# Attention stage of a two-layer mixture kernel: order of the operand splits, spread of the score matmuls, number format of the second mix, engine of the remainders

## The chip, the cores and the metric

One core of a Trainium2 chip runs the whole program. The metric is device time in microseconds (us): the median of several executions. The profile is of one more execution, read by the hardware profiler. Engines: TensorE (PE, its weight loads PEld), VectorE (DVE), ScalarE (ACT), GpSimd (POOL), and SyncE (SP), which here only issues transfers (DMAs).

## What is computed

Attention with mixing over heads, then two feed-forward layers. Batch 4, 12 heads, 448 positions, head size 64. Cut to what matters here:

```python
scores = scale * np.matmul(q, k.transpose(0, 1, 3, 2))
scores = np.einsum('bhij,hg->bgij', scores, w_pre)      # first mix, over heads
attn = np.exp(scores - np.max(scores, axis=-1, keepdims=True))
attn = attn / (np.sum(attn, axis=-1, keepdims=True) + 1e-09)
attn = np.einsum('bgij,gk->bkij', attn, w_post)         # second mix
return np.matmul(attn, v)                               # then x @ w_in, tanh, @ w_out, experts
```

Inputs are float32. The kernel keeps float32 accuracy by writing an operand as a 16-bit high part and a 16-bit remainder and adding up products of the parts.

## The kernel before

The change lies in `attention` alone. What it does is cut into 180 **steps**, 45 for each of the four batches b. A step takes ten query positions with all twelve heads, 120 rows. A batch has four tiles of queries (`TILES`, t = 0 to 3) of 12, 12, 12 and 9 steps; a step is (b, t, c), and its number is 45 b + 12 t + c.

For step s the program writes, in this order:

- `shuffle` (L220): a transfer `G<-S` that gathers the 120 rows of the step out of the score tile S. SP runs its list in order, and four G buffers rotate (`GB`), so the transfer for step s + 4 can start when the first mix of step s has read its G.
- `premix` (L236): the first mix on TensorE (L240, float32, two passes, 120x448), the row minimum on VectorE (L244), for a halved step a bias add (L248), the exponential on ScalarE with its row sum (L250). A **halved** step (`halved`, L90) scales its exponentials, and GpSimd makes the 16-bit remainder of them (L255).
- whatever `at(s, ...)` put down for step s (the table `todo`): `scores`, and the loading and splitting of operands.
- `after` (L391): every second step `normalise` (L258: add an epsilon L265, reciprocal L266, then the second mix's weights `wr`, one instruction L272 for a float32 step, two, L276 and L277, for a halved one), then `postmix` (L281) of step s - 4 (`LAG`): the second mix on TensorE (L290: 8 matmuls in float32 or 12 in 16 bits), the copy out of PSUM on ScalarE (L294), the remainder on GpSimd (L295).

`scores(b, t, p)` (L195) makes the scores of two heads for a whole tile, six matmuls (L203), and copies them to S: one copy in three on VectorE (L207), the others on ScalarE (L209). Six such calls make a tile, p = 0 to 5; they run while the tile before is being mixed (L388).

Operands are loaded into one pool of three buffers, `raw` (`p3`):

- v of a batch, four parts: `fetch_v` (L183), then `split_v` (L186): the high part on ScalarE (L192), the remainder on GpSimd (L193), 128x768.
- q and k of the next batch, three double pairs of heads: `fetch_pairs` (L168) and `split_pairs` (L179): per load a high part on ScalarE (L175, 128x896) and two remainders (L177, 128x448), one on VectorE and one on GpSimd.
- the first feed-forward weights, `fetch_w` and `convert_w` (three conversions and a remainder on VectorE, L77 to L81 and L327).

When a batch's last step is mixed, `window` (L355) runs `values` (L298): 24 matmuls for each two heads, about 14 us of TensorE, with conversions of weights between. The window of batch b stands behind step 45 (b + 1) + 3.

PSUM banks: scores 0 and 1, first mix 2, 3 and 6 in turn, second mix and values 4 and 5. The five exponential tiles A rotate too (`LAG + 1`).

The order on each engine is not that of the text: a scheduler orders the instructions at compile time by its own estimates and the dependencies, and each engine then runs its list strictly in order. Code behind the attention stage is the same in both kernels, and so is its order from the last steps of batch 3 on.

## Time and profile before

| | us |
|---|---|
| median of 3 runs | 1286.94 (1285.57 to 1294.75) |
| the profiled execution | 1288.26 |
| its span, first to last instruction | 1286.0 |
| TensorE busy | 1193.8 (93%) |
| VectorE busy | 855.1 (66%) |
| ScalarE busy | 729.0 (57%) |
| GpSimd busy | 707.3 (55%) |

The attention stage takes the first 470 us. How to read the rows below: a stretch A:B is in us from the first instruction; `(x310)` counts instructions; PEclk is the granted TensorE clock as a share of full speed; in a timeline, the bracket at the end of a row is the engine's idle time just before it and what ended it. A busy TensorE is modelled and holds its pipelining; start to start is its pace.

### The profile page before, as it was taken

The page shows a single profiled execution, that of the slowest core. Times are in us where ns is not written, and L with a number is a line of the kernel's source. Part 1 is how long each engine was busy: PE and PEld are TensorE (multiplying, and loading weights), DVE is VectorE, ACT ScalarE, POOL GpSimd, SP SyncE. Part 2 cuts the span into 40 slices and gives each one's busy share as a digit, 9 for nine tenths or more (in the row PEclk, how much of TensorE's full clock was granted, in tenths as well). Part 3 has the DMA queues.
Part 4 walks back from the last instruction along what each step waited for, and adds up shares of the span by engine and source line. Part 5 has one row for each costly group of instructions (what it writes and reads, how often), then busy time and mean ns, then how long its engine had stood idle before and what let it go on. Part 6 is the DMA issues. An engine that isn't in the chain of part 4 may idle for free.

```text
span 1286.0 us, 23742 instructions
## 1 busy us (share of the span) xinstructions
PE 1193.8 (93%) x8624; PEld 837.4 (65%) x8648; DVE 855.1 (66%) x1895; ACT 729.0 (57%) x1499; POOL 707.3 (55%) x594
## 2 busy tenths in 40 slices
PE   8999899989999988999899999999978899999995
PEld 3655565555555664566566666667876678989883
DVE  5877687768767829977766456745878345566662
ACT  6777687667767744444455444545556334555551
POOL 5887678577767753433443335334566355566550
PEclk8999999999999999999999999999998999999998
DMA  6555746555574476223001000100043656678640
GB/s 212 174 182 146 221 162 190 175 182 184 148 208 162 116 236 219 93 97 131 25 1 50 1 25 1 50 1 1 2 140 133 212 194 205 213 242 263 229 159 22
DMA packets 82854, 173.90 MB, mean 135 GB/s; under 512 B 12155, under 2 KB 60155, under 8 KB 82728
## 3 DMA queue, kind: packets, MB, share of 16 engines
q1 hardware_dynamic: 76986, 160.75, 38.7%
q0 software_dynamic: 5472, 11.43, 3.0%
q8 instruction: 70, 1.15, 0.4%
q14 instruction: 56, 0.46, 0.1%
q10 hardware_dynamic: 270, 0.12, 0.0%
HBM read 110.79 MB, written 23.30 MB: 104 GB/s over the span
## 4 chain that ended last, share of the span: by engine, by line
PE 59%; DVE 16%; DMA 12%; ACT 6%; issue 3%; POOL 2%; SPq 0%; POOLq 0%; ACTq 0%; DVEq 0%
PE bank L561 11%; PE bank L533 10%; PE bank L913 7%; PE bank L240 7%; PE bank L937 7%; PE bank L290 7%; DMA G<-S 3%; PE bank L203 3%; DMA raw_v<-in_v_dram 3%; PE bank L305 2%; DVE g L547 2%; DMA wor<-in_w_out_dram 2%; DVE g L548 2%; DVE wl_a L903 2%; ACT A L250 1%
## 5 line engine op out<-in xcount | busy, mean ns | idle before, releaser
L561 PE MATMUL bank<-ghl,whl 128*128 128x512 f32 (+1 forms) x1152 | 258.1, 376 | 9.3 <-POOL ghl L551 4.9
L561 PEld LDWEIGHTS bank<-ghl,whl 128*128 128x128 f32 x1152 | 199.6, 192 | 50.8 <-POOL ghl L551 6.3
L483 POOL TENSOR_TENSOR whl<-wo,whl 128x768 fp32r<-128x768 f32 x64 | 118.8, 1857 | 177.2 <-ACT whl L482 177.1
L295 POOL TENSOR_TENSOR at<-at 128x480 f16<-128x480 f32 x180 | 177.0, 996 | 51.9 <-ACT at L294 50.2
L240 PE MATMUL bank<-G,wmix 120*120 120x448 f32 x360 | 176.7, 575 | 11.3 <-DMA G<-S 11.3
L290 PE MATMUL bank<-wr,A 120*128 120x120 f32 (+4 forms) x1800 | 175.3, 246 | 5.2 <-ACT x L312 3.0
L250 ACT ACTIVATE A<-bank,st 120x448 f32<-120x448 f32 x180 | 114.3, 636 | 53.5 <-DVE st L244 22.2
L244 DVE TENSOR_REDUCE st<-bank 120x1 f32<-120x448 f32 x180 | 111.2, 618 | 46.3 <-PE bank L240 45.1
L903 POOL TENSOR_TENSOR wl_a<-wr_a,wh_a 128x768 bf16<-128x768 f32 x56 | 93.1, 1670 | 70.4 <-ACT wh_a L902 70.0
L551 POOL TENSOR_TENSOR ghl<-g,ghl 128x512 fp32r<-128x512 f32 (+1 forms) x64 | 76.6, 1197 | 99.7 <-ACT ghl L550 99.7
L903 DVE TENSOR_TENSOR wl_a<-wr_a,wh_a 128x768 bf16<-128x768 f32 x56 | 83.1, 1484 | 61.9 <-ACT wh_a L902 61.9
L533 PEld LDWEIGHTS <-wih 128*128 128x128 f16 x768 | 72.4, 99 | 76.3 <-issue 15.9
L290 PEld LDWEIGHTS bank<-wr,A 120*128 120x128 f32 (+1 forms) x720 | 94.5, 198 | 34.5 <-issue 17.8
L294 ACT COPY at<-bank 128x480 f32<-128x480 f32 x180 | 101.3, 567 | 25.0 <-PE bank L290 24.7
L902 ACT CAST wh_a<-wr_a 128x768 f16<-128x768 f32 x112 | 92.6, 829 | 39.2 <-PE bank L937 35.2
L543 DVE SCALAR_TENSOR_TENSOR g<-bank,u 128x512 f32<-128x512 f32 (+1 forms) x64 | 39.9, 623 | 108.6 <-ACT d L540 105.2
L255 POOL TENSOR_TENSOR A<-A 120x448 f16<-120x448 f32 (+1 forms) x90 | 84.4, 938 | 32.0 <-ACT A L250 13.4
L482 ACT CAST whl<-wo 128x768 fp32r<-128x768 f32 x64 | 53.1, 831 | 71.1 <-PE bank L561 53.0
L533 PE MATMUL bank<-mxh,wih 128*128 128x512 f16 (+1 forms) x384 | 85.1, 358 | 5.4 <-DVE d L544 4.2
L290 PEld LDWEIGHTS <-A 120*128 120x128 bf16 (+2 forms) x1080 | 63.1, 100 | 40.9 <-issue 33.9
L550 ACT CAST ghl<-g 128x512 fp32r<-128x512 f32 (+1 forms) x64 | 36.2, 566 | 91.6 <-DVE g L548 81.0
L913 PE MATMUL bank<-xph_a,wh_a 128*128 128x208 f16 (+5 forms) x336 | 87.2, 262 | 0.0
(214 smaller groups left out, 2701.3 us busy)
## 6 DMA issues: line engine op xcount, KB each, us to landing
wr_a<-in_w_dram SPq DMA_DIRECT2D x64, 768.0 KB
G<-S SPq DMA_DIRECT2D x176, 210.0 KB
raw_w<-in_w_in_dram SPq DMA_DIRECT2D x32, 384.0 KB
wor<-in_w_out_dram SPq DMA_DIRECT2D x16, 768.0 KB
raw_v<-in_v_dram SPq DMA_DIRECT2D x16, 384.0 KB
yg<-row SPq DMA_DIRECT2D x3, 1540.0 KB
raw_q<-in_q_dram SPq DMA_DIRECT2D x9, 448.0 KB
raw_k<-in_k_dram SPq DMA_DIRECT2D x9, 448.0 KB
```

Of the source, the lines that this page charges most:

```text
L240: nc.tensor.matmul(ps[:r, :S], wmix[:r, :r], g[:r], start=True, stop=True)
L244: nc.vector.tensor_reduce(out=st[:r, k:k + 1], in_=ps[:r, :S], axis=AX.X, op=ALU.min)
L250: nc.scalar.activation(out=a[:r, :S], in_=ps[:r, :S], func=AF.Exp, bias=bias, scale=-1.0, accum_out=st[:r, 4 + k:5 + k])
L290: nc.tensor.matmul(ps[:, jc * r:jc * r + r], x[:r, js], w[:r].rearrange("p (a b) -> p a b", b=10)[:, :, :n], start=(i == 0), stop=(i == le ...
L294: nc.scalar.copy(at32[:, :, t0:t0 + n], v)
L295: nc.gpsimd.tensor_tensor(out=atl[:, :, t0:t0 + n], in0=at32[:, :, t0:t0 + n], in1=ath[:, :, t0:t0 + n], op=ALU.subtract)
L483: nc.gpsimd.tensor_tensor(out=w[:, 1], in0=wo[f], in1=w[:, 0].bitcast(F32), op=ALU.subtract)
L533: nc.tensor.matmul(h, u[f][:, c], X[b][v][:, c, :N], start=(i == 0), stop=(i == len(seq) - 1))
L561: nc.tensor.matmul(Y[b][c][:, :N], w[:, u, 128 * c:128 * c + 128], hl[:, v, :N], start=(f == 0 and i == 0), stop=(f == FC - 1 and i == 2))
L902: nc.scalar.copy(wh, raw)
L903: (nc.vector if j else nc.gpsimd).tensor_tensor(out=wl, in0=raw, in1=wh, op=ALU.subtract)
L913: nc.tensor.matmul(h, w[u][:, 128 * c:128 * c + 128], XP[e][v][:, c, :N], start=(i == 0), stop=(i == len(seq) - 1))
```

## The change

1. `halved`: two steps in three (all but every third) instead of every second are mixed a second time in 16 bits; the table of epsilons has six columns instead of two.
2. `split` and `split_v`: all remainders of loaded q, k and v go to VectorE; before, GpSimd made half of those of q and k, and all of v.
3. `behind`: the splits of v, q, k and the conversions of weights are tied behind the row minimum and the exponential of the step in whose slot they stand (`latest`), and they come first in the slot. Two loads (`fetch_v`, `fetch_pairs`) come four steps ahead of their split; before, that was four for v and two for q and k. Splits of v move from steps 5, 9, 13, 17 of a batch to 9, 13, 17, 21; those of q and k from 25, 29, 33 to 27, 31, 35.
4. `scores` of the next tile lie within eight steps of a tile of twelve (two steps ahead of the tile to six behind its start) instead of twelve; the gathering transfers may start three steps ahead of a tile instead of two.

```diff
 def halved(u):
-    return u % 2 == 1
+    return u % 3 != 0
@@ split
-            for p, eng in enumerate((nc.vector, nc.gpsimd)):
-                eng.tensor_tensor(out=lo[:, 2 * u + p, s0:], in0=raw[:, p], in1=hi[:, 2 * u + p, s0:], op=ALU.subtract)
+            for p in range(2):
+                nc.vector.tensor_tensor(out=lo[:, 2 * u + p, s0:], in0=raw[:, p], in1=hi[:, 2 * u + p, s0:],
+                                        op=ALU.subtract)
@@ split_v
-            nc.gpsimd.tensor_tensor(out=vl[:, jc], in0=raw, in1=vh[:, jc], op=ALU.subtract)
+            nc.vector.tensor_tensor(out=vl[:, jc], in0=raw, in1=vh[:, jc], op=ALU.subtract)
@@ premix
-            nc.vector.tensor_reduce(out=st[:r, k:k + 1], in_=ps[:r, :S], axis=AX.X, op=ALU.min)
+            latest["dve"] = nc.vector.tensor_reduce(out=st[:r, k:k + 1], in_=ps[:r, :S], axis=AX.X, op=ALU.min)
-            nc.scalar.activation(out=a[:r, :S], in_=ps[:r, :S], func=AF.Exp, bias=bias, scale=-1.0,
-                                 accum_out=st[:r, 4 + k:5 + k])
+            latest["act"] = nc.scalar.activation(out=a[:r, :S], in_=ps[:r, :S], func=AF.Exp, bias=bias, scale=-1.0,
+                                                 accum_out=st[:r, 4 + k:5 + k])
@@ the table of steps
+        def behind(f, *a):
+            with ExitStack() as order:
+                for x in latest.values():
+                    order.enter_context(tc.issue_after(x.ins))
+                f(*a)
-                at(s0 + 1 + 4 * jc, fetch_v, b, jc)
-                at(s0 + 5 + 4 * jc, split_v, b, jc)
+                at(s0 + 9 + 4 * jc, behind, split_v, b, jc)
+                at(s0 + 5 + 4 * jc, fetch_v, b, jc)
+                    at(s0 + 27 + 4 * u, behind, split_pairs, b + 1, u)
                     at(s0 + 23 + 4 * u, fetch_pairs, b + 1, u)
-                    at(s0 + 25 + 4 * u, split_pairs, b + 1, u)
-                at(45 * b + 10 + 7 * k, fetch_w, u)
-                at(45 * b + 13 + 7 * k, convert_w, u)
+                at(45 * b + 7 + 7 * k, fetch_w, u)
+                at(45 * b + 12 + 7 * k, behind, convert_w, u)
-                    at(s0 - 3 + (2 * p + 1) * ng // H if ti else 2 * p - AHEAD, scores, *tiles[ti + 1], p)
+                    at(s0 - 2 + 8 * p * ng // 60 if ti else 2 * p - AHEAD, scores, *tiles[ti + 1], p)
@@ the loop over steps
-            while nxt < min(s + GB, len(steps)) and first[steps[nxt][:2]] <= s + 2:
+            while nxt < min(s + GB, len(steps)) and first[steps[nxt][:2]] <= s + 3:
-            for f, a in todo.pop(s, []):
+            for f, a in sorted(todo.pop(s, []), key=lambda x: x[0] is not behind):
```

Three places show what this does to the engines' lists. Names carry batch, tile and step: `G_1_0_10` is the gather of batch 1, tile 0, c = 10, step 55; `raw_v_1_3` is the last part of v of batch 1.

**The last load of v in batch 1, on SP and on ScalarE.** Before, SP issues it behind the gather of step 55, which waits for the first mix of step 51:

```order
L231 DMA G_1_0_9_1989<-S_1_0_1225 120x1x448
L133 DMA raw_w_9_2109<-in_w_in_dram 128x384
L231 DMA G_1_0_10_2022<-S_1_0_1225 120x1x448
L133 DMA raw_v_1_3_2200<-in_v_dram 128x768
L133 DMA raw_w_10_2321<-in_w_in_dram 128x384
L231 DMA G_1_0_11_2043<-S_1_0_1225 120x1x448
```

and on ScalarE its use (the last row) stands behind the exponential of step 52 (`A2`), in front of that of step 53:

```order
L209 COPY S_1_1_1517<-bank1_196_1998 120x448
L294 COPY at32_97<-bank5_197_2007 128x48x10
L294 COPY at32_97<-bank4_199_2036 128x48x10
L250 ACTIVATE A2_107,st_26_2026<-bank3_198_2024,st_26_2026 120x448
L192 CAST vh_1_1969<-raw_v_1_3_2200 128x768
```

In the change SP issues it behind the gather of step 63 (`G_1_1_6`), which waits for the first mix of step 59:

```order
L133 DMA raw_w_10_2344<-in_w_in_dram 128x384
L358 DMA wind0_59<-wh_9_2278 128x384
L358 DMA wind1_60<-wl_9_2279 128x384
L232 DMA G_1_1_6_2371<-S_1_1_1598 120x1x448
L133 DMA raw_v_1_3_2437<-in_v_dram 128x768
L232 DMA G_1_1_7_2401<-S_1_1_1598 120x1x448
```

and its use is tied to step 66. From issue to use there was one step before; there are seven now. Steps are counted from the one whose first mix lets the issue go to the one behind whose exponential the use stands. Counted this way over the whole list, the loads of v had 0 to 4 steps before wherever they were not held over from the batch ahead, and have 5 to 18 now. Loads of q and k had 1 or 2 steps for the second and third k, and have 5 to 7 for the first double pair, 3 to 5 for the second, and 2, 1 and 2 for the third (batches 1, 2 and 3).

**VectorE where the first pairs are split, batch 0.** The rows start at the row minimum that stands ahead of the second-mix weights of step 24. Before:

```order
L244 TENSOR_REDUCE st_13_994<-bank6_110_992 120x1
L265 TENSOR_TENSOR st_12_932<-st_12_932,bank7_1_98 120x2
L266 RECIPROCAL st_12_932<-st_12_932 120x2
L272 TENSOR_SCALAR wr_24_1009<-bank7_1_98,st_12_932 120x120
L207 COPY S_0_3_876<-bank1_112_998 88x448
L276 TENSOR_SCALAR wr_25_1011<-bank7_1_98,st_12_932 120x120
L277 SCALAR_TENSOR_TENSOR wr_25_1011<-bank7_1_98,st_12_932,wr_25_1011 120x120
```

With the change, the four remainders of the pairs stand in a row, and this is the row minimum of step 28, not of step 26:

```order
L245 TENSOR_REDUCE st_14_1119<-bank3_118_1117 120x1
L273 TENSOR_SCALAR wr_24_1064<-bank7_1_98,st_12_983 120x120
L277 TENSOR_SCALAR wr_25_1066<-bank7_1_98,st_12_983 120x120
L177 TENSOR_TENSOR ql_119<-raw_q_1_0_950,qh_118 128x448
L278 SCALAR_TENSOR_TENSOR wr_25_1066<-bank7_1_98,st_12_983,wr_25_1066 120x120
L177 TENSOR_TENSOR ql_119<-raw_q_1_0_950,qh_118 128x448
L177 TENSOR_TENSOR kl_121<-raw_k_1_0_952,kh_120 128x448 x2
```

**TensorE at the same step.** In both kernels the second mix of step 24 stands behind the first mix of step 28, with one call of scores between. Here the list of the change from the end of that call to the second mix (its first row of four matmuls):

```order
L204 LDWEIGHTS qh_118
L204 MATMUL bank0_119_1126<-kl_121,qh_118 88x448
L204 LDWEIGHTS qh_118
L204 MATMUL bank1_120_1127<-kl_121,qh_118 88x448
L291 MATMUL bank4_121_1143<-wr_24_1064,A4_109 128x120 x4
```

So the weights of step 24 were two row minima ahead of their use, and are none ahead now. Counted over all 180 steps: before, 5 steps have no row minimum between, 9 have one, 70 two and 96 three or four; with the change 19 have none, 52 one, 60 two and 49 three or four. In the change 26 couples of score matmuls (the two heads of a call, on two halves of the array) no longer stand side by side, 10 of them in steps 24 to 39, three in batch 1, 10 in steps 114 to 129, three elsewhere.

## Rows read from the trace of the kernel before

**Rows 1.** Busy us by stretch: length, PE, PEld, DVE, ACT, POOL, clock, DMA.

```profile
20.20:66.50 46.30, 46.30 (x310) 26.86 (x311) 35.54 (x105) 33.12 (x83) 30.81 (x31) 0.94 0.54 180
66.50:115.50 49.00, 45.05 (x326) 27.60 (x324) 38.31 (x109) 37.24 (x88) 38.43 (x38) 0.97 0.59 171
115.50:183.40 67.90, 63.54 (x506) 38.97 (x504) 49.10 (x136) 47.22 (x113) 47.25 (x47) 0.97 0.58 182
183.40:230.40 47.00, 44.14 (x327) 26.56 (x327) 37.62 (x106) 36.93 (x87) 37.45 (x38) 1.00 0.61 180
230.40:299.70 69.30, 64.60 (x508) 39.28 (x505) 48.86 (x133) 46.58 (x111) 46.66 (x46) 0.98 0.57 179
299.70:348.40 48.70, 44.98 (x326) 27.69 (x324) 37.84 (x109) 37.14 (x87) 38.75 (x38) 0.96 0.60 173
348.40:416.70 68.30, 63.15 (x506) 38.91 (x504) 49.38 (x136) 47.84 (x115) 47.57 (x47) 0.98 0.58 182
416.70:456.00 39.30, 35.50 (x263) 22.88 (x264) 30.59 (x90) 27.30 (x69) 28.50 (x30) 1.00 0.44 121
42.70:66.50 23.80, 23.80 (x183) 14.66 (x181) 20.48 (x61) 18.40 (x46) 17.11 (x18) 1.00 0.47 162
512.00:544.00 32.00, 28.52 (x127) 18.47 (x130) 30.63 (x38) 12.39 (x21) 14.38 (x8) 1.00 0.26 93
```

**Rows 2.** Waits in 20 to 456 us: total us, times, longest.

```profile
ACT vh L192 <- DMA raw_v<-in_v_dram: 13.3, 10, 2.7
PE bank L240 <- DMA G<-S: 11.3, 12, 2.3
ACT kh L175 <- DMA raw_k<-in_k_dram: 7.7, 3, 2.8
```

**Rows 3.** Timeline of TensorE without a stall, tiles 1 and 2 of batch 0.

```profile
65.88 0.79 PE L290 MATMUL bank<-wr,A 120*128 120x120 f16 x12
66.51 0.97 PE L240 MATMUL bank<-G,wmix 120*120 120x448 f32 x2
67.41 0.39 PE L203 MATMUL bank<-kh,qh 64*88 64x448 f16 x2
...
68.10 1.15 PE L290 MATMUL bank<-wr,A 120*128 120x120 f32 x8
69.09 0.92 PE L240 MATMUL bank<-G,wmix 120*120 120x448 f32 x2
```

**Rows 4.** Timeline of TensorE in the first window and behind it.

```profile
124.13 1.79 PE L305 MATMUL bank<-at,vh 128*64 128x448 bf16 x16
...
126.55 1.75 PE L305 MATMUL bank<-at,vh 128*64 128x448 bf16 x16
...
140.29 0.79 PE L290 MATMUL bank<-wr,A 120*128 120x120 f16 x12 [1.00 <-ACT x L312]
```

**Rows 5.** VectorE by line and form, 0 to 470 us: busy us, mean ns, idle before.

```profile
L177 DVE TENSOR_TENSOR kl<-raw_k,kh 128x448 f16<-128x448 f32 x9 | 8.0, 893 | 8.2 <-ACT kh L175 8.2
L177 DVE TENSOR_TENSOR ql<-raw_q,qh 128x448 f16<-128x448 f32 x9 | 7.2, 801 | 1.8 <-ACT qh L175 1.8
L277 DVE SCALAR_TENSOR_TENSOR wr<-bank,st,wr 120x120 bf16<-120x120 f32 x88 | 29.7, 338 | 1.7
L248 DVE TENSOR_SCALAR st<-st 120x1 f32<-120x1 f32 x88 | 13.2, 150 | 1.4
L244 DVE TENSOR_REDUCE st<-bank 120x1 f32<-120x448 f32 x176 | 108.8, 618 | 43.4 <-PE bank L240 42.2
```

**Rows 6.** Timelines of VectorE and GpSimd at remainders, alone and together.

```profile
70.25 0.63 DVE L177 TENSOR_TENSOR ql<-raw_q,qh 128x448 f16<-128x448 f32 x1 [0.20 <-ACT qh L175]
...
80.11 1.03 POOL L177 TENSOR_TENSOR kl<-raw_k,kh 128x448 f16<-128x448 f32 x1 [1.39 <-ACT kh L175]
80.12 1.50 DVE L177 TENSOR_TENSOR kl<-raw_k,kh 128x448 f16<-128x448 f32 x1 [2.95 <-ACT kh L175]
...
1058.66 0.96 DVE L903 TENSOR_TENSOR wl_a<-wr_a,wh_a 128x768 bf16<-128x768 f32 x1 [2.03 <-ACT wh_a L902]
```

More of the change, by code (lines that the diff above doesn't have):

```diff
@@ L110, in attention @@
         lasting = bank(7, 0, 1)
-        wmul, eps, cw = lasting[:, :120], lasting[:120, 120:122], lasting[:, 512 - HW:]
+        wmul, eps, cw = lasting[:, :120], lasting[:120, 120:126], lasting[:, 512 - HW:]
         wpost = cp.tile([120, 120], F32, tag="wpost", name="wpost")
@@ L232, in shuffle @@
             G[b, t, c] = g
-        mid, sums = {}, {}
+        mid, sums, latest = {}, {}, {}
         def premix(b, t, c, u):
@@ L264, in normalise @@
                 v = st[:r, 4:6][:, ks]
-                nc.vector.tensor_tensor(out=v, in0=v, in1=eps[:r, ks], op=ALU.add)
+                nc.vector.tensor_tensor(out=v, in0=v, in1=eps[:r, us[0] % 6:us[0] % 6 + 2][:, ks], op=ALU.add)
                 nc.vector.reciprocal(out=st[:r, 6:8][:, ks], in_=v)
@@ L401, in attention @@
         nc.vector.tensor_copy(wmul[:120], wpost)
-        for i in range(2):
+        for i in range(6):
             nc.vector.memset(eps[:, i:i + 1], 1e-9 * (AS if halved(i) else 1.0))
```

## The prediction, made before the changed kernel was run

> **What bounds the kernel now.** I read the busy times by stretch first. In 42.70:66.50, one tile of twelve steps, TensorE is busy in all 23.80 us and VectorE in 20.48 [rows 1]: TensorE is the pace, VectorE has 14% to spare. So I cut attention into its eight stages. Four hold the first half of a batch and the window of the batch ahead (I call them V; the first has no window): 46.30, 67.90, 69.30 and 68.30 us long. Three hold tiles 2 and 3, where q and k are split (P): 49.00, 47.00 and 48.70. A last one (T) takes 39.30 [rows 1]. TensorE is idle for 4.4, 4.7 and 5.1 us in the three later V, and for 4.0, 2.9 and 3.7 in P. VectorE's busy time is 77 to 80% of P, so it is not the bound there either. What TensorE waits for stands in the table of waits: 11.3 us in 12 waits for a gather G, and behind it ScalarE, 13.3 us in ten waits for a load of v and 7.7 in three for one of k [rows 2]. ScalarE stands still with the exponentials and score copies queued behind it, the score tile S is finished late, and its gather G after that. Those are the stalls that the longer leads can remove.
>
> **Change part by part.** I work against the profiled execution, 1288.26; the median of the runs shown is 1.3 lower.
>
> *Number format.* Start to start, a 16-bit second mix costs TensorE 66.51 - 65.88 = 0.63 us, a float32 one 69.09 - 68.10 = 0.99 [rows 3]. Two more steps of each twelve are halved, each -0.36: a tile at TensorE's pace goes from 23.8 to 23.1. On VectorE each newly halved step adds 0.338 (L277) and 0.150 (L248) [rows 5], together 0.49.
>
> *V stages at TensorE's pace.* Two tiles, 46.2; a window of six pairs of heads at 126.55 - 124.13 = 2.42, 14.5; and 1.0 of idle time behind the window for ScalarE's last conversion (the row at 140.29) [rows 4]: 61.7. The first V has no window: 46.3 - 1.4 = 44.9. This takes all waits for v as gone, since its loads get 5 to 18 steps where most had 0 to 4, and a step is about 2 us.
>
> *VectorE in V.* The four remainders of v come to VectorE, between a batch's steps 9 and 22, 14 steps. The trace has no such instruction on VectorE. The nearest of its shape, 128x768, took 0.96 beside an idle GpSimd [rows 6]. Upper bound: a 128x448 remainder took 0.63 alone and 1.50 where GpSimd's own began at the same moment [rows 6]; 0.96 and the same 0.87 on top are 1.83. I take 1.2 (why, below). VectorE's work in 14 steps is then 14/12 x 20.48 = 23.9, plus 14/6 x 0.49 = 1.1, plus 4 x 1.2 = 4.8: 29.8. An engine whose list is in strict order and waits on others doesn't get to 100%: VectorE was 86% busy where it was not the bound (20.48 of 23.80) and 96% where it was the busiest engine, late in the program (30.63 of 32.00) [rows 1]. I choose 92% between them: 32.4 us for these steps. The second-mix weights were mostly two or more row minima ahead, and this lead can be eaten up: two steps of it, an estimate, 3 us. So 29.4 against 27.0 of TensorE (14/12 x 23.1): 2.4 per V. The first V becomes 47.3 (+1.0), the others 64.1 (-3.8, -5.2, -4.2). V together: -12.2.
>
> *VectorE in P.* Three double pairs of q and k are six loads; each had one remainder on VectorE and one on GpSimd, so six more come over. The price of a pair is bounded by 0.63 and 1.50 [rows 6]; the mean of eighteen is 0.85 (893 and 801 ns) [rows 5]. I take 0.95, since GpSimd loses its own remainder at that moment but has more halved steps' remainders to write; the same 0.3 above the lone time makes the v remainder 1.2. Six new ones cost 5.7, six old ones 0.6 more, 3.5 more halved steps 1.7: +8.0 on 38.31, 37.62 and 37.84 [rows 1], so 46.3, 45.6 and 45.8. Over 0.92, less the 3 us of lead: 47.3, 46.6, 46.8. TensorE alone would need 43 to 44 (its busy time of 44.1 to 45.1, less 3.5 x 0.36), so VectorE sets P: -1.7, -0.4, -1.9, together -4.0.
>
> *The rest.* The third q and k of batch 2 have one step from issue to use, where the others have two or more: a stall of the old kind (7.7/3 = 2.6 us on ScalarE for one of k [rows 2], of which I give 2.0 to TensorE): +2.0. In T, 3.5 x 0.36: -1.2. The narrower spread of the scores puts S in place earlier; I give it nothing of its own, since the gathers' waits are already taken as gone in V, and in P VectorE hides it. Without that cover P could not fall below TensorE's 43 to 44. The tie `behind` holds a split back for at most a step; with the loads of v 5 steps early it costs nothing, and where the lead is short it is in the 2.0.
>
> Sum: -12.2 - 4.0 + 2.0 - 1.2 = -15.4. 1288.3 - 15.4 = 1272.9 for a profiled execution; less 1.3, **1272** for the median.
>
> **Rivals.**
>
> *A. TensorE is the pace everywhere.* VectorE's lead takes up the added work, since over a whole batch it is well below 100%. V: -1.4, -6.2, -7.6, -6.6. P at 43.5: -5.5, -3.5, -5.2. T: -1.2. Together -37.2, **1250**. For it: VectorE still idles a fifth of P. Against it: the added work stands in four or five steps around each split, not over the stage; in the change's list the four remainders stand among the weights of steps 24 and 25, which TensorE wants next.
>
> *B. VectorE becomes the bound, slower than before.* Each remainder on VectorE meets one on GpSimd and waits for it: the pair's at 1.50, v's at 1.83 [rows 6]. P: 6 x 1.50 + 6 x 0.65 + 1.7 = +14.6, so 52.9, 52.2 and 52.4 of work, 54.5, 53.7 and 54.0 long: +17.5. V: 23.9 + 1.1 + 7.3 = 32.3, over 0.92 less 3 is 32.1, 5.1 beyond TensorE: +3.7 in the first, -1.1, -2.5 and -1.5 in the others, -1.4. With +2.0 and -1.2 that is +16.9, **1304**. Between 0.95 and 1.50 the sum moves by 32.3, 5.9 us for each 0.1, so the sign turns where the pair's mean price reaches 1.21 (v's about 1.5). For it: the row at 80.12, where two remainders that began together took 1.03 on GpSimd and 1.50 on VectorE [rows 6]. Against it: the mean of 0.85 though half of the work was on GpSimd at just that moment.
>
> The Trainium skill, "SBUF — State Buffer", section "SBUF: two separate sides", speaks for B: VectorE and GpSimd share a pair of ports as an exclusive lock, and a VectorE instruction with two SBUF inputs waits for a GpSimd one that holds it, whole. The pair at 80.11 agrees: 1.50 is about 0.63 behind most of 1.03. By that rule a remainder costs its own time and what is left of GpSimd's instruction; how often that is much, only a run can show.
>
> *C. The order loses what the loads win.* In the list of before 5 second mixes have their weights written with no row minimum in between, all among the last steps; in the change's list 19, of which 13 are new and in front of the last ten steps. There TensorE, done with the first mix of the same step, must wait for a row minimum (0.618) and two writes of weights (0.338 each) [rows 5]: 1.3 us, 13 times, 17. With the main sum -15.4 + 17: about **1289**. For it: the order is strict. Against it: a call of scores often stands between, and part of these steps lies in stretches that I already put down to VectorE. 26 broken couples of score matmuls have no price in the trace; they are bounded by nothing and, if a second half then runs alone for its 0.39 [rows 3], by 26 x 0.39 = 10. I take nothing, as P is VectorE's by my sum; the upper end leads to C.
>
> **How the numbers follow.** Main case 0.48, its own range 1260 to 1282 (pair's price 0.8 to 1.1, VectorE's share 0.90 to 0.95). A 0.15, B 0.15, C 0.22. The range 1251 to 1298 leaves out half of A, two thirds of B and a little of the main case, together 0.2. 1% is about what a measurement of this kernel can tell from no change. Faster by over 1% is below 1274.1: some 0.58 of the main case, A, and a little of C, 0.45. Slower is above 1299.8: most of B and a little of C, 0.13. Within 1%: 0.42.
>
> **What would show it.** In the profile after, ScalarE's waits for loads of v should be gone or below 2 us, and TensorE's waits for G with them. The V stages with a window should be near 64 us, P near 47 with VectorE busy 95% or more of the stretch around the splits, and TensorE's waits in P should name VectorE. The remainders' mean shows which case it is: 0.95 for the main one, under 0.8 and TensorE busy all through for A, over 1.2 for B. For C, waits of TensorE for second-mix weights about 1.3 us long, at a dozen places outside the splits. The prediction is wrong if the waits for loads stay (then the leads that I counted in steps don't hold in time), or if VectorE's extra work moves nothing (A).

## The result, and the profile after

The changed kernel took **1274.14 us** (median of 4 runs, 1271.63 to 1274.84) against 1288.12 for the kernel before (4 runs); the ratio is 0.988, interval 0.984 to 0.992. 14 us, 1.1%, were gained; 1272 had been forecast. The profiled execution took 1271.63, its span 1269.8 (1286.0 before): 16.2 us shorter, of which 14.7 lie between the first mix of step 0 and that of step 179.

The stages of the changed kernel, cut at the first mixes of steps 0, 24, 45, 69, 90, 114, 135, 159 and 179, by busy time (columns as in [rows 1]; the rows are V0, P0, V1, P1, V2, P2, V3 and T):

```profile
20.66:64.48 43.82, 43.55 (x300) 24.95 (x300) 35.95 (x103) 32.55 (x80) 30.46 (x32) 0.94 0.46 155
64.48:116.52 52.04, 48.04 (x365) 28.46 (x365) 46.94 (x135) 39.59 (x94) 36.93 (x38) 1.00 0.63 186
116.52:179.61 63.09, 61.58 (x512) 37.50 (x508) 52.55 (x143) 46.38 (x111) 42.86 (x45) 1.00 0.61 190
179.61:227.59 47.98, 45.14 (x352) 26.99 (x351) 42.00 (x125) 38.37 (x90) 36.24 (x38) 1.00 0.62 184
227.59:287.20 59.61, 59.21 (x499) 36.71 (x496) 48.99 (x131) 43.79 (x106) 42.43 (x45) 1.00 0.60 187
287.20:341.53 54.33, 50.93 (x365) 30.37 (x365) 46.20 (x134) 39.57 (x93) 37.00 (x38) 0.94 0.60 177
341.53:404.63 63.10, 61.58 (x512) 37.50 (x508) 52.66 (x143) 46.45 (x111) 43.10 (x45) 1.00 0.61 191
404.63:441.59 36.96, 34.26 (x281) 21.94 (x281) 31.60 (x99) 27.89 (x71) 32.14 (x35) 1.00 0.48 134
sum 420.93, PE 404.28 PEld 244.43 DVE 356.88 ACT 314.60 POOL 301.15; mean PE 50.54 PEld 30.55 DVE 44.61 ACT 39.32 POOL 37.64
```

Against [rows 1] every V is shorter (by 2.5, 4.8, 9.7 and 5.2) and every P longer (by 3.0, 1.0 and 5.6). Of the 22.2 us that V gained, P gave back 9.6; some 5 us of both is a border that moved (below). The waits, in 20 to 440 us, answer to [rows 2]; for loads only one of 1.8 us is left, and none for v:

```profile
PEld bank L241 <- DMA G<-S: 2.9, 2, 2.5
PE bank L241 <- DMA G<-S: 2.1, 3, 1.0
ACT kh L175 <- DMA raw_k<-in_k_dram: 1.8, 1, 1.8
```

VectorE by line and form, 0 to 470 us, answering to [rows 5]: all remainders are here now. A pair's costs 0.83 in the mean (652 and 1009 ns), v's 1.17:

```profile
L194 DVE TENSOR_TENSOR vl<-raw_v,vh 128x768 bf16<-128x768 f32 x16 | 18.6, 1165 | 1.2 <-ACT vh L193 1.0
L177 DVE TENSOR_TENSOR kl<-raw_k,kh 128x448 f16<-128x448 f32 x18 | 17.7, 1009 | 0.8 <-ACT kh L175 0.8
L177 DVE TENSOR_TENSOR ql<-raw_q,qh 128x448 f16<-128x448 f32 x18 | 11.4, 652 | 0.3 <-ACT qh L175 0.2
```

What makes P0 and P2 long shows best at step 32, batch 0. On VectorE, the row minimum (L245), then four remainders in a row, and only then the bias add (L249) that the exponential waits for:

```profile
87.35 0.62 DVE L245 TENSOR_REDUCE st<-bank 120x1 f32<-120x448 f32 x1 [0.17 <-PE bank L241]
87.89 1.30 DVE L177 TENSOR_TENSOR ql<-raw_q,qh 128x448 f16<-128x448 f32 x2
89.11 2.73 DVE L177 TENSOR_TENSOR kl<-raw_k,kh 128x448 f16<-128x448 f32 x2
91.77 0.14 DVE L249 TENSOR_SCALAR st<-st 120x1 f32<-120x1 f32 x1
```

ScalarE (first row) and TensorE (second row) behind it:

```profile
92.00 0.63 ACT L251 ACTIVATE A<-bank,st 120x448 f32<-120x448 f32 x1 [2.14 <-DVE st L267]
92.78 1.01 PE L241 MATMUL bank<-G,wmix 120*120 120x448 f32 x2 [1.94 <-ACT A L251]
```

The minimum was known at 87.97, its bias add ran at 91.77; TensorE's next first mix had no free bank until the exponential had read one. The same block stands in batch 2 (310.61 to 314.49), with the same 1.94 us of TensorE behind it. The tie holds a split behind the minimum and exponential of its own step, 31; in VectorE's list its remainders come behind the minimum of step 32 too, and that step is halved and needs a bias add, which stands behind them. Such a block is not always dear: those at steps 28, 73 and 118, where 3.7 to 3.9 us also lie between minimum and bias add, cost TensorE single waits of 0.36, 0.99 and 0.36.

### The profile page after: what moved, and what is told of

Its sections match the earlier page's. It is cut to its first block, busy times and chain, and to the rows that moved or that the text cites. A ratio compares the mean times of both kernels' runs of the same rounds, so it can differ in the third digit from the quotient of the medians.

```text
span 1269.8 us, 24112 instructions
## 1 busy us (share of the span) xinstructions
PE 1190.3 (94%) x8768; PEld 830.2 (65%) x8768; DVE 887.4 (70%) x1996; ACT 728.7 (57%) x1499; POOL 689.4 (54%) x587
## 4 chain that ended last, share of the span: by engine, by line
PE 59%; DVE 21%; DMA 7%; ACT 7%; issue 4%; POOL 1%; SPq 0%; DVEq 0%; POOLq 0%; ACTq 0%
PE bank L569 11%; PE bank L541 10%; PE bank L921 7%; PE bank L945 7%; PE bank L291 7%; PE bank L241 6%; PE bank L306 4%; PE bank L204 3%; DMA wor<-in_w_out_dram 2%; DVE wl_a L911 2%; DVE g L555 2%; DVE g L556 2%; DVE st L245 2%; ACT A L251 2%; DMA G<-S 1%
## 5 line engine op out<-in xcount | busy, mean ns | idle before, releaser
L569 PEld LDWEIGHTS bank<-ghl,whl 128*128 128x128 f32 x1152 | 199.5, 191 | 52.1 <-POOL ghl L559 6.4
L296 POOL TENSOR_TENSOR at<-at 128x480 f16<-128x480 f32 x180 | 182.5, 1023 | 61.1 <-ACT at L295 60.1
L241 PE MATMUL bank<-G,wmix 120*120 120x448 f32 x360 | 172.0, 569 | 7.8 <-ACT A L251 4.3
L291 PE MATMUL bank<-wr,A 120*128 120x120 f16 (+2 forms) x1920 | 165.0, 234 | 5.9 <-DVE wr L273 2.4
L256 POOL TENSOR_TENSOR A<-A 120x448 f16<-120x448 f32 x120 | 114.6, 957 | 49.7 <-ACT A L251 49.2
L251 ACT ACTIVATE A<-bank,st 120x448 f32<-120x448 f32 x180 | 115.2, 640 | 41.2 <-DVE st L249 21.9
L245 DVE TENSOR_REDUCE st<-bank 120x1 f32<-120x448 f32 x180 | 111.1, 617 | 33.5 <-PE bank L241 32.7
L291 PEld LDWEIGHTS <-A 120*128 120x128 bf16 (+2 forms) x1440 | 83.3, 98 | 55.5 <-issue 37.1
L945 PE MATMUL bank<-rh_a,wh_a 128*128 128x208 f16 (+5 forms) x336 | 86.6, 261 | 0.0
L945 PE MATMUL bank<-rh_a,wl_a 128*128 128x208 f16 (+5 forms) x336 | 86.6, 261 | 0.0
```

The costliest lines, as they stand in the source:

```text
L241: nc.tensor.matmul(ps[:r, :S], wmix[:r, :r], g[:r], start=True, stop=True)
L245: latest["dve"] = nc.vector.tensor_reduce(out=st[:r, k:k + 1], in_=ps[:r, :S], axis=AX.X, op=ALU.min)
L251: latest["act"] = nc.scalar.activation(out=a[:r, :S], in_=ps[:r, :S], func=AF.Exp, bias=bias, scale=-1.0, accum_out=st[:r, 4 + k:5 + k])
L256: nc.gpsimd.tensor_tensor(out=parts[1][:r, :S], in0=a[:r, :S], in1=parts[0][:r, :S], op=ALU.subtract)
L291: nc.tensor.matmul(ps[:, jc * r:jc * r + r], x[:r, js], w[:r].rearrange("p (a b) -> p a b", b=10)[:, :, :n], start=(i == 0), stop=(i == le ...
L296: nc.gpsimd.tensor_tensor(out=atl[:, :, t0:t0 + n], in0=at32[:, :, t0:t0 + n], in1=ath[:, :, t0:t0 + n], op=ALU.subtract)
```

## Experiments

Twelve kernels. **Theory 1**: the loads shorten V. **T1**: blocks of work in front of a bias add lengthen P. **T2**: VectorE's amount of work does. **T3**: couples of scores that stand apart do. In the table, ratio and interval are against the kernel before in the same job. Attention is from the first mix of step 0 to that of step 179; TensorE's idle time is this length less its busy time; scores and second mix are TensorE's time from the start of one matmul to that of the next, all of one profiled execution each. The last column adds up 2 us times (1 - granted clock) over 20 to 444 us: TensorE's time given up to a lower clock at most.

| kernel | median us | ratio, interval | attention | idle | scores | second mix | clock |
|---|---|---|---|---|---|---|---|
| before | 1288.12 | 1 | 435.6 | 28.5 | 65.8 | 142.3 | 11.6 |
| the change | 1274.14 | 0.988, 0.984 to 0.992 | 420.9 | 16.6 | 72.9 | 134.6 | 6.5 |
| e1 order only | 1268.45 | 0.984, 0.977 to 0.992 | 414.3 | 13.6 | 66.8 | 138.9 | 5.3 |
| e2 no tie | 1271.46 | 0.986, 0.979 to 0.994 | 418.6 | 18.3 | 70.6 | 132.0 | 3.1 |
| e3 pairs half on GpSimd | 1270.88 | 0.986, 0.978 to 0.993 | 419.0 | 17.8 | 69.5 | 133.4 | 6.8 |
| e4 every second halved | 1270.15 | 0.985, 0.977 to 0.992 | 414.1 | 11.0 | 68.9 | 138.3 | 2.9 |
| e5 casts ahead | 1271.91 | 0.989, 0.986 to 0.993 | 419.4 | 14.8 | 72.0 | 134.8 | 7.5 |
| e6 order, two of three | 1270.05 | 0.988, 0.985 to 0.992 | 412.7 | 21.9 | 64.8 | 129.3 | 4.8 |
| e7 order, new spread | 1269.48 | 0.989, 0.986 to 0.992 | 412.9 | 11.0 | 69.5 | 138.3 | 1.7 |
| e8 old spread | 1266.88 | 0.986, 0.979 to 0.993 | 412.7 | 17.6 | 67.6 | 130.9 | 1.7 |
| e9 all as before on GpSimd | 1273.30 | 0.984, 0.980 to 0.988 | 422.8 | 21.4 | 68.6 | 134.6 | 12.7 |
| e10 e9, pairs untied | 1280.64 | 0.989, 0.983 to 0.994 | 423.1 | 23.9 | 68.2 | 133.3 | 8.5 |
| e11 e9, casts ahead | 1276.16 | 0.988, 0.983 to 0.993 | 414.4 | 20.1 | 65.8 | 132.7 | 3.4 |
| e12 other phase | 1279.54 | 0.994, 0.991 to 0.997 | 423.1 | 17.6 | 74.4 | 133.6 | 12.1 |

Three limits to read it by. Every interval overlaps that of the change (e12's only at its edge, 0.991 to 0.992): by the total, no variant can be told apart from it. One kernel's executions differ (e5's lay between 1264.51 and 1276.79), and the profiled one can lie at an end of them: e7's was the lowest of ten times (1260.01), those of e3, e9 and e10 the highest of four (1274.95, 1279.72 and 1281.70). So an attention length that differs from another's by less than some 5 us, and for e7 and e9 by less than 10, isn't yet a difference between kernels. And the stages don't hold the same instructions everywhere: in the change, e3 and e5, P0 and P2 hold two second mixes and a call of scores more than in e2 and e6, some 2.3 us of TensorE (before, e1, e4 and e7 have the border of e6). What follows rests on waits and rows, and on totals only where they speak.

**e1: the order alone.** The kernel before, with `behind`, `latest` and the new slots; everything else as before:

```diff
-                at(s0 + 1 + 4 * jc, fetch_v, b, jc)
-                at(s0 + 5 + 4 * jc, split_v, b, jc)
+                at(s0 + 9 + 4 * jc, behind, split_v, b, jc)
+                at(s0 + 5 + 4 * jc, fetch_v, b, jc)
...
+                    at(s0 + 27 + 4 * u, behind, split_pairs, b + 1, u)
                     at(s0 + 23 + 4 * u, fetch_pairs, b + 1, u)
-                    at(s0 + 25 + 4 * u, split_pairs, b + 1, u)
```

> The kernel before with the order part of the change alone (tie behind, new slots of fetches and splits); number format, engines of the remainders and spread of the scores as before. Theory 1: the stages V were shortened by the loads, so V with a window falls to 62 to 65 us (67.9, 69.3 and 68.3 before; 63.1, 59.6 and 63.1 with the change), ScalarE's wait for raw_v is below 2 us, P stays at 47 to 49, and the total is 1270 to 1275. Rival: V became short because VectorE took the remainders of v or because of the number format; then V stays within 1.5 us of before and the total is 1283 or more.

Theory 1 holds, the total was even lower than it said. No wait of ScalarE for a load is left in 20 to 440 us (21.0 before, [rows 2]), TensorE's idle time fell from 28.5 to 13.6 us, and V with a window fell to 62.5, 62.5 and 62.1, TensorE busy in all but 0.4 to 0.8 us of it, with v's remainders still on GpSimd. The first P and the V behind it:

```profile
67.99:115.51 47.52, 44.54 (x322) 26.90 (x323) 38.20 (x107) 37.47 (x87) 38.72 (x38) 1.00 0.64 187
115.51:177.98 62.47, 61.63 (x506) 37.73 (x505) 48.99 (x136) 47.10 (x113) 46.27 (x46) 1.00 0.61 192
```

So the order alone brings as much as the whole change: nothing that the other three parts add shows in the total. The three V with a window are 18.5 us shorter than before. About 5 of these are stretches at a lower clock that stood behind waits there (last section); the other 13.5 stand beside 12.0 us of ScalarE's waits for v in these stages. How such a wait reaches TensorE, two rows of the kernel before show, in P0, for a load of k: ScalarE stands still, copies the scores late (80.93), and TensorE waits for the bank that this copy empties:

```profile
79.09 0.94 ACT L175 CAST kh<-raw_k 128x896 f16<-128x896 f32 x1 [2.63 <-DMA raw_k<-in_k_dram]
81.50 0.78 PE L203 MATMUL bank<-kh,qh 64*88 64x448 f16 x2 [2.13 <-ACT S L209]
```

From the first mix of step 0 to that of step 179, TensorE waited 12.7 us for score copies before and not at all in e1. For gathers it waited 9.0 before and 11.7 in e1: in V with a window these went (4.5 to 0), in P they came up (0.6 to 6.6).

**e2: no tie.**

```diff
-            with ExitStack() as order:
-                for x in latest.values():
-                    order.enter_context(tc.issue_after(x.ins))
-                f(*a)
+            f(*a)
```

> The change without the tie (the splits keep their slots and come first in them, but nothing holds them behind the step's row minimum and exponential). Theory 1: the tie makes the lead, so the scheduler pulls the splits forward again, ScalarE waits 8 us or more for raw_v, V with a window is 65 us or more, total 1280 or more. Rival: the new slots make the lead and the tie only costs in P, where it puts the four remainders between a row minimum and its bias add; then V stays within 1 us of the change, P falls by 2 us or more each, total 1266 or less.

Each theory was half right. ScalarE's waits for loads are back, those for v almost whole:

```profile
ACT vh L193 <- DMA raw_v<-in_v_dram: 12.8, 12, 2.0
ACT qh L175 <- DMA raw_q<-in_q_dram: 3.4, 3, 1.6
ACT kh L175 <- DMA raw_k<-in_k_dram: 3.2, 4, 1.0
```

and V with a window is 64.8, 65.0 and 65.0: 1.1, 3.1 and 1.3 above the change with the border put back (63.7, 61.9 and 63.7). So the tie makes the lead for v. But it costs in P: 47.7, 46.1 and 47.9 without it, against 49.7, 47.4 and 52.0 in the change with the border put back; by the list no block of four stands in front of a bias add. The two add up to nearly nothing in the total. What Theory 1 doesn't explain: ScalarE waits 18.2 us for loads in attention, nearly as in the kernel before (20.2), and yet attention is 17.0 us shorter than there. No wait of TensorE between 28 and 432 us reaches 1 us here, and no stretch there has a lower clock. So it is not the sum of ScalarE's waits that costs, but what of it reaches TensorE.

**e3: half of the pairs' remainders back on GpSimd.**

```diff
-            for p in range(2):
-                nc.vector.tensor_tensor(out=lo[:, 2 * u + p, s0:], in0=raw[:, p], in1=hi[:, 2 * u + p, s0:],
-                                        op=ALU.subtract)
+            for p, eng in enumerate((nc.vector, nc.gpsimd)):
+                eng.tensor_tensor(out=lo[:, 2 * u + p, s0:], in0=raw[:, p], in1=hi[:, 2 * u + p, s0:], op=ALU.subtract)
```

> The change with one remainder of each load of q and k back on GpSimd (v's stay on VectorE). Theory 2: P is long because VectorE is the bound there; six remainders fewer at a mean of 0.83 take 5 us off its work in each P, so P falls from 52.0, 48.0 and 54.3 to 47 to 48, 44 to 46 and 48 to 49, total about 1262. Rival: P is long for the score couples that the order broke on TensorE; then P stays within 1.5 us each, total 1270 or more.

The forecast of Theory 2 was missed: P0, P1 and P2 were 52.2, 47.1 and 52.1, though six remainders had left VectorE (42.9 us of work in P0 for 46.9). A clean test of T2 it isn't. The wait of 1.94 is gone as well, and in its place a load of k comes late in each P: in P0 ScalarE waits 1.61 for it at 98.03 and TensorE 2.18 for a score copy at 99.92, with a lower clock from 102 to 106 behind it.

**e4: every second step halved, all else as changed.**

```diff
-    return u % 3 != 0
+    return u % 2 == 1
```

> The change with every second step halved as before. If the number format is worth 0.36 us a step where TensorE is the pace, V is longer by 1.4 each, and P, bound by VectorE, shorter by its 1.7 of work there: together +0.5 to +1.5, total about 1275. If TensorE is the pace in P too, P is longer by 1.2 each: total 1284. If VectorE is the pace in V as well, V is shorter: total 1270 or less.

None of the three was met: V with a window was 63.4 to 63.8, so not shorter than in the change, yet the total is 1270.15; P fell to 46.5, 46.4 and 46.1, with all remainders on VectorE (P0, P1, P2):

```profile
68.53:115.08 46.55, 44.61 (x327) 27.18 (x323) 40.07 (x116) 37.23 (x89) 31.02 (x33) 1.00 0.63 188
178.50:224.93 46.43, 44.27 (x328) 26.59 (x327) 41.15 (x117) 36.81 (x86) 31.38 (x33) 1.00 0.63 185
288.73:334.83 46.10, 44.57 (x326) 27.32 (x323) 39.89 (x116) 37.16 (x88) 31.42 (x33) 1.00 0.65 190
```

VectorE has 0.8 to 4.3 us more work than in e1, and P is no longer than there: the remainders on VectorE don't lengthen P by themselves. Between T1 and T2 e4 doesn't decide, since against the change it also has less of VectorE's work in P (40.1 for 46.9 in P0, border included), and its steps 28, 32, 118 and 122 are float32, without a bias add behind the block. In attention as a whole, the remainders, the new spread and GpSimd's relief cost or bring nothing that shows (414.1 against 414.3).

**e5: the same work, behind the bias add.** Casts stay in their slots; the four remainders go one step later, tied to that step's bias add (so does what else is tied in a halved step, splits of v and conversions of weights):

```diff
-                nc.vector.tensor_scalar(out=bias, in0=st[:r, k:k + 1], scalar1=EXPB, scalar2=None, op0=ALU.add)
+                latest["dve"] = nc.vector.tensor_scalar(out=bias, in0=st[:r, k:k + 1], scalar1=EXPB, scalar2=None, op0=ALU.add)
...
                     at(s0 + 27 + 4 * u, behind, split_pairs, b + 1, u)
+                    at(s0 + 28 + 4 * u, behind, rest_pairs, b + 1, u)
```

> The change, with the casts of q and k on ScalarE in their slots as before, but the four remainders in the slot one step later, tied behind the bias add of that step where it is halved. The same work on every engine; in VectorE's list no block of four remainders stands between the row minimum of steps 28, 32, 73, 118 and 122 and their bias adds. Theory T1: the block kept the exponential, and TensorE behind it, waiting; TensorE's idle time in attention falls from 16.6 us to 11 or less, P0 and P2 are 3 us or more shorter, total 1269 or less. Rival T2: VectorE's amount of work is the bound in P; idle time and P stay within 1.5 us, total 1272 to 1275. Rival T3: the score couples that don't stand side by side are the cost; there are about as many as in the change, so the scores keep their 72 to 73 us of TensorE and the total is 1272 or more.

At the two places it did what T1 says, and not in the total. VectorE at the same split, now with the bias add (L260) ahead of the block:

```profile
88.66 0.62 DVE L256 TENSOR_REDUCE st<-bank 120x1 f32<-120x448 f32 x1
89.20 0.15 DVE L278 RECIPROCAL st<-st 120x2 f32<-120x2 f32 x1
89.32 0.15 DVE L260 TENSOR_SCALAR st<-st 120x1 f32<-120x1 f32 x1
89.40 1.16 DVE L184 TENSOR_TENSOR ql<-raw_q,qh 128x448 f16<-128x448 f32 x2
90.48 2.68 DVE L184 TENSOR_TENSOR kl<-raw_k,kh 128x448 f16<-128x448 f32 x2
```

TensorE's wait of 1.94 is gone in both batches; 0.85 is left, for the weights behind the block (93.56, from DVE wr L284). P0 and P2, with the border of the change and nearly its work on VectorE (45.0 us each), fell from 52.0 and 54.3 to 50.1 each; of the second fall up to 3.4 is a stretch at a lower clock (last section). This is the cleanest evidence for T1 and against T2. In P1, where the change has no such wait, a new one of 2.23 for a score copy came up (213.72) and two stretches at a lower clock, and P1 took 55.2. Its length also holds 31 second-mix matmuls and six of scores that other kernels have in V. The cause of that wait is open.

**e6: order and number format.** e1 with `halved` of the change (the six epsilons are in e1 already):

```diff
-    return u % 2 == 1
+    return u % 3 != 0
```

> The order part alone as in e1, and two steps in three halved; engines of the remainders and spread of the scores as before. Theory F1: the number format is worth its 0.36 us a step where the order leaves TensorE the pace; 30 more halved steps bring 5 to 10 us, total 1259 to 1264, and the second mix falls from 138.8 us of TensorE to 134 or less. Rival F2: the added weights and bias adds on VectorE, 30 times 0.49, use it up; the total stays at 1268 +- 2. Rival F3: as in the change against e4, the number format costs 4 us: 1272.

F1 is right on TensorE's own time and wrong on the total; F2's total is the nearest, its cause isn't shown. The second mix fell by 9.6 us (30 steps at 0.32), but TensorE's idle time rose by 8.3. First row e6, second row e1, TensorE's waits for a gather in 60 to 440 us:

```profile
PE bank L240 <- DMA G<-S: 15.3, 15, 2.4
```
```profile
PE bank L240 <- DMA G<-S: 10.1, 11, 2.3
```

A quicker TensorE waits longer for S and its gathers. P took 47.1, 46.4 and 46.6 with 42.4 to 42.7 us of TensorE in it, and 47.5, 46.8 and 46.8 with 44.3 to 44.6 in e1: it isn't TensorE that sets P. Which engine does isn't settled; none is busy for all of it.

**e7: order and new spread.** e1 with these two lines:

```diff
-                    at(s0 - 3 + (2 * p + 1) * ng // H if ti else 2 * p - AHEAD, scores, *tiles[ti + 1], p)
+                    at(s0 - 2 + 8 * p * ng // 60 if ti else 2 * p - AHEAD, scores, *tiles[ti + 1], p)
...
-            while nxt < min(s + GB, len(steps)) and first[steps[nxt][:2]] <= s + 2:
+            while nxt < min(s + GB, len(steps)) and first[steps[nxt][:2]] <= s + 3:
```

> The order part alone as in e1, and the new spread of the scores; engines of the remainders and number format as before. TensorE waited for gathers 20 us or more in e1 by the table of waits (12.8 and 11.4). Theory: the earlier scores take these waits away: below 8 us for G, total 1262 to 1265. Rival: the waits for G are the first mix waiting for TensorE's own work of another stage, they turn into others; total 1268 +- 2. What it differs from e4 by is the price of the remainders on VectorE: under the theory e4 is 5 us longer, under the rival 2.

TensorE's waits for G fell only to 8.0 (from 12.8, 20 to 440 us), its idle time by 2.6; the scores took 2.7 us more of TensorE. The rival is nearer: 1269.48. A price of the remainders on VectorE doesn't show against e4 (412.9 and 414.1 of attention).

**e8: the change with the old spread** (the two lines of e7 the other way round).

> The change with the spread of the scores (and the start of the gathers) of before. It leaves 10 couples apart where the change has 15 by the same count, and blocks of remainders in front of the bias adds of 32, 77 and 122 only. Theory T1: three late bias adds instead of five bring 2 to 4 us, total 1270 to 1272. Rival T3: five couples fewer bring 2 us and the waits for G come back with 5 or more, total 1277 or more.

The median is below what both said, but the profile speaks for neither alone: TensorE idles as long as in the change (17.6 against 16.6); it is the scores (67.6 against 72.9) and the clock that are better. Its longest wait of TensorE in 22 to 430 us is 1.06, where the change has 1.94 twice and 1.78 once. And the block that cost 1.94 there stands here too, at the same step 32, with 3.79 us between minimum and bias add as there, and costs 0.70:

```profile
86.07 2.73 DVE L177 TENSOR_TENSOR kl<-raw_k,kh 128x448 f16<-128x448 f32 x2
88.72 0.14 DVE L249 TENSOR_SCALAR st<-st 120x1 f32<-120x1 f32 x1
89.45 0.35 PE L204 MATMUL bank<-kh,qh 64*120 64x448 f16 x1 [0.70 <-DVE S L208]
```

While the block runs, TensorE has two first mixes, two second mixes and three score matmuls to do here and is busy to 88.75. In the change it has one second mix less, is done at 90.84, a microsecond before the bias add, and then waits for the exponential too. So T1 holds for a place, not for every block.

**e9 to e11: remainders on the engines of before**, number format and spread as changed:

```diff
-            for p in range(2):
-                nc.vector.tensor_tensor(out=lo[:, 2 * u + p, s0:], in0=raw[:, p], in1=hi[:, 2 * u + p, s0:],
+            for p, eng in enumerate((nc.vector, nc.gpsimd)):
+                eng.tensor_tensor(out=lo[:, 2 * u + p, s0:], in0=raw[:, p], in1=hi[:, 2 * u + p, s0:], op=ALU.subtract)
...
-            nc.vector.tensor_tensor(out=vl[:, jc], in0=raw, in1=vh[:, jc], op=ALU.subtract)
+            nc.gpsimd.tensor_tensor(out=vl[:, jc], in0=raw, in1=vh[:, jc], op=ALU.subtract)
```

e10 and e11 undo the block of e9's two remainders in front of three bias adds, the first by leaving the pairs untied, the second by the edit of e5:

```diff
-                    at(s0 + 27 + 4 * u, behind, split_pairs, b + 1, u)
+                    at(s0 + 27 + 4 * u, split_pairs, b + 1, u)
```

> The change with the remainders of q, k and v on the engines of before; order, spread and number format as changed. Attention from the first to the last first mix took 420.9 us in the change, 414.1 in e4 and 412.9 in e7. Theory I: only VectorE's remainders on top of the number format make the loss; without them the second mix keeps 134 us or less of TensorE, its idle time falls to 12 us or less, attention takes 410 or less, total 1260 to 1265. Rival II: the new spread and the number format lose it together, whatever the engine (e3 was 419.0 with half of the remainders back); attention 416 or more, total 1269 or more.

> As e9, and the splits of q and k without the tie (v's and the weights' keep it). The two remainders that stand between row minimum and bias add in steps 28, 73 and 118 of e9 are gone there. Theory T1 (a block in front of a bias add costs): attention 1 to 4 us shorter than e9. Rival: the loads of q and k come late again without the tie; ScalarE waits 5 us or more for raw_q and raw_k, attention 1 us or more longer than e9.

> As e9, with the remainders of q and k one step behind their casts and tied behind the bias add, as in e5. By the same count no block and no broken couple is left in it. Theory T1: attention 2 to 4 us shorter than e9. Rival T2 (amount of work): the same within 1 us. Rival: the remainders hold the raw buffers a step longer, and the loads behind them come late; ScalarE waits for raw_q and raw_k, attention longer.

Theory I falls: without any extra remainder on VectorE attention was no shorter, and the numbers of Rival II were met. In e9 TensorE waited five times for 1.6 to 2.95 us, for score copies and gathers, and the clock was low behind four of the five. e10 raised ScalarE's waits for loads of k and q from 6.4 to 10.1 us and brought no gain. e11 was 8.4 us shorter in attention, but the clock column alone fell by 9.3, and the total doesn't tell e9, e10 and e11 apart. In the profiles, kernels with the new spread and the number format together mostly have 418.6 to 423.1 us of attention (e11 414.4), those with one of them 412.7 to 414.1. With e7 profiled at the low end of its times and e3, e9 and e10 at the high end of theirs, it isn't shown that this pattern is one of the kernels, and no cause of it is shown.

**e12: the blocks made longer.**

```diff
-    return u % 3 != 0
+    return u % 3 != 2
```

> The change with the float32 step of every three moved on by two (steps 2, 5, 8 in place of 0, 3, 6); as many halved steps, the same work. By the list blocks of remainders and conversions in front of a bias add are longer (estimated 4 to 6 us at steps 28, 36, 73, 81, 118 and 126), and 10 couples of scores stand apart where the change has 15 by the same count. Theory T1 (the blocks cost): TensorE waits for the exponential or the bias add 1.5 us or more in at least four of these places, its idle time in attention is 19 us or more, attention 423 or more against 420.9. Rival T3 (the couples cost): the scores take 71 us or less of TensorE against 72.9, attention 419 or less.

Attention was 423.1, and by the ratio this is the slowest of the twelve, as T1 said, but not by the mechanism that it named: idle time rose by 1.0 only, and the longest waits name a gather (2.05 and 1.83) and a score copy (2.04). They stand between minimum and bias add of steps 36, 126 and 81, where the blocks are; how these would delay a gather isn't shown. T3's count by the list falls: fewer couples apart, yet 74.4 us of scores; in the trace more score matmuls run alone here than in the change (79 for 75, below). What is larger is the clock's column, by 5.6.

The lowest medians are e8's and e1's. Against the change their intervals overlap, so none is shown to beat it; e1 does with the order alone what the change does with four parts.

## Why the prediction was right, and where its terms were off

The total was right (1272 for 1274.14, gain 15.4 forecast against 14.7 in attention), and the mechanism named first, late loads that ScalarE waits for, is shown by e1, with the limit that e2 sets. That the sum came out so close is luck: V was shorter than forecast and P longer, by about as much, in part through a border and in part through waits and a clock that the sum didn't have.

| | before | forecast | measured |
|---|---|---|---|
| V, four stages | 251.8 | 239.6 | 229.6 |
| P, three stages | 144.7 | 140.7 and 2.0 for a late load | 154.3 |
| T, to step 179's first mix | 39.1 | 37.9 | 37.0 |

- **A border that moved.** Part of these differences is no time at all. P0 and P2 hold 244 second-mix matmuls and 78 of scores in the change, 224 and 72 in e6; V0 and V2 hold 20 second-mix ones less than there (192 and 236), V1 and V3 12 less (244 for 256), P1 and T 12 more. Two steps at 0.63 and 0.99 and a score call at about 0.7 make 2.3 us, one halved step makes 0.6: some 5 us moved from V to P, and 0.6 to T. The prediction cut both kernels at the same steps and didn't read from the order that the second mix lags differently there.
- **V.** Put back, V0 is 46.1, V1 and V3 are 63.7, V2 is 61.9 (forecast 47.3 and 64.1, without VectorE's drag 44.9 and 61.7). So the term at TensorE's pace is near, and the drag of 2.4 is too high in V0 and absent in V2. In V1 and V3 there are 2.0 above that pace, but that VectorE makes them isn't shown: TensorE idles 1.5 us there, and e7, with the remainders of v on GpSimd, took 65.2, 63.2 and 63.7. The price of a v remainder was right (1.17 for 1.2).
- **The path to TensorE.** The prediction led from a late load over a late S to its gather, and took the gathers' waits as gone with the loads. In V that is so. In P the late loads cost through the score banks, and with early loads (e1) waits for gathers came up instead; they fall to 8.0 with the earlier scores of e7 and to 2.1 in the change, where the prediction gave the spread nothing of its own.
- **P.** The price of a pair's remainder was 0.83 for 0.95. VectorE's work was 46.9, 42.0 and 46.2 for 46.3, 45.6 and 45.8, the border's part in it. With the border put back, P was 49.7, 47.4 and 52.0 for 47.3, 46.6 and 46.8. What lies above has names: 1.94 us in P0 and in P2 is the wait behind the block, 1.78 in P1 the late load, and P2 has also a stretch at half clock behind its wait, up to 3.4. The 3 us of lead did not help there, because what was late was the bias add of one step, not the weights that have the lead. Without these P is 47.8, 45.6 and 46.7, near the forecast. Its reason, that VectorE's work sets P, isn't borne out. VectorE was 90, 88 and 85% busy over P and nearly all the time around the splits, as the prediction had it:

```profile
80.00:96.00 16.00, 13.71 (x108) 8.49 (x106) 15.61 (x40) 11.79 (x29) 12.49 (x13) 1.00 0.70 212
```

But P took 45.6 to 47.5 in e1, e4, e6 and e7 too, with 37 to 41 us of VectorE's work. So "over 0.92, less the 3 us of lead" gave the right size without being the cause; what sets P at 46 to 47 is open.

- **The late load** was right in place and size: 1.82 us of ScalarE at 209.41, 1.78 of TensorE at 210.83, for 2.0. It came in P1.
- **The number format** was 0.36 a step; e6 measured 0.32, but as a gain it doesn't exist in e6, since the gathers don't come sooner. In the change the second mix fell by 7.7 us and the scores rose by 7.1.
- **The couples** had no price in the sum. At 68.16 in the change a half of a couple runs alone for 0.38, as the upper bound said; in P0 78 score matmuls took 12.1 us (0.155 each), where the kernel before needed 9.0 for 72 (0.125). The trace gives the price: from the first mix of step 0 to that of step 179, 75 score matmuls start alone in the change (no other one within 0.06 us) and 22 before. One alone takes TensorE 0.27 us to its next matmul in the mean, idle time left out, one of a couple 0.12. So 53 more alone, at 0.15 each, are enough for the 7.1 us that the scores rose by. In all fourteen kernels one of a couple takes 0.117 to 0.121, and the scores' time goes with the number alone (14 in e6, 79 in e12). The expectations of e8 and e12 count 15 apart in the change by another count of the list than the 26 above; neither count gave the time.
- **The rivals.** A's gains for V summed to 21.8, and 22.2 were measured, but with the border put back it is 16.4, between A and the main sum. B had the direction of P, but not its cause: the remainders' mean price of 0.83 (kl 1.01, ql 0.65) stayed below the 1.21 at which B's sum turns, and e4 shows P short with all of them on VectorE. The rule of the Trainium skill ("SBUF — State Buffer", section "SBUF: two separate sides") that stood beside B agrees with single rows again: the k remainders at 89.11 took 2.73 for two while GpSimd worked from 89.05 to 91.37, where one at 210.38 took 0.62 beside an idle GpSimd. It doesn't decide the time. C, second mixes without a row minimum of slack, is not seen: between 22 and 440 us TensorE idled for weights once for 0.99 us and otherwise for 0.36 or less, where 13 waits of 1.3 had been put.

## What to carry to other kernels

When an operand's split is placed in a strict order, tie it behind work of its step so that its load has time, and then read what the tie pushes it in front of: a 0.14 us instruction behind a block of four remainders cost TensorE as much as a late load in two places, and little where TensorE had other work in its list. Before adding up stage by stage, count in the new order which instructions changed stage. And give a stage's time to an engine's share of work only if that engine's waits say so; undo the parts one by one, since here one part of four brought as much as the whole.

## What the runs showed of the hardware

Behind most long waits of TensorE the granted clock fell, and TensorE then paid a second time. In the fourteen profiles TensorE waited 31 times for 1.6 us or more between 28 and 432 us; soon behind 19 of these waits the clock fell. Of the 20 stretches at a lower clock in that time, 19 stand behind such a wait and one behind a wait of 1.36 (e5, 195.14). The prediction had waits at their own length. In the change, P2, in stretches of 2 us, right behind the wait of 1.94 that ended at 315.50:

```profile
315.50:317.50 2.00, 2.00 (x8) 1.55 (x9) 1.90 (x6) 2.00 (x6) 1.88 (x2) 0.69 0.91 263
317.50:319.50 2.00, 2.00 (x7) 1.03 (x6) 1.88 (x5) 0.63 (x2) 1.44 (x2) 0.50 0.62 214
319.50:321.50 2.00, 2.00 (x14) 1.60 (x14) 0.00 (x0) 1.83 (x4) 1.09 (x2) 0.50 0.13 44
321.50:323.50 2.00, 2.00 (x9) 0.54 (x7) 0.93 (x2) 2.00 (x5) 0.43 (x2) 0.60 0.00 0
323.50:325.50 2.00, 2.00 (x8) 0.97 (x6) 2.00 (x6) 0.94 (x3) 1.07 (x1) 1.00 0.60 135
```

The clock is at its lower level, 1.2 of 2.4 GHz, from about 316 to 323, with TensorE busy all through; VectorE has nothing to do for 2 us. That stretch gave up 3.4 us. The same wait of 1.94 in batch 0 had no such stretch behind it (P0's clock is 1.00), so a wait doesn't make it sure. In the kernel before, five such stretches, each giving up 1.6 to 1.7 us, lie behind waits of 1.70 to 2.25 (those that end at 81.50, 154.26, 274.17, 314.77 and 374.16), 8.4 us in all; behind a sixth, of 1.94 at 391.90, there is none. e1 has none from 28 to 430 us, though it waited 2.31 at 96.36. So some of the gain of earlier loads is the clock's: in the kernel before, a stall of 2 us was worth up to 3.7. Between the variants it is the clock column that spreads most, 1.7 to 12.7.
